# A causal convolution and a gated feed-forward block: the first convolution of blocks 4 and 5 moved from TensorE to ACT, DVE and POOL

## The chip, the cores and the metric

The kernel runs on one core of a Trainium2 chip. The metric is the device time of one execution in microseconds (us), median of several runs. The engines are called TensorE (PE in the profile, with its weight loads as PEld), VectorE (DVE), ScalarE (ACT), GpSimd (POOL) and SyncE (SP, which only issues DMAs here).

## What is computed

A softmax over 7 taps for each of 8 heads, a causal depthwise convolution of x (8 sequences of 4096 tokens, 192 channels, each head's taps on its 24 channels), and a gated feed-forward block with 1536 hidden units on the result.

```python
w = np.exp(weight - weight.max(-1, keepdims=True))
w = w / (w.sum(-1, keepdims=True) + 1e-09)                  # 8 heads x 7 taps
x_pad = np.concatenate([zeros(B, 6, D), x], axis=1)
out[b, s, h] = sum(w[h, k] * x_pad[b, s + k, h] for k in range(7))
g = out @ w_gate                                           # 192 -> 1536
val = out @ w_val
y = (g / (1 + np.exp(-g)) * val) @ w_out                   # 1536 -> 192, 32768 tokens
```

## The kernel before

**Blocks, steps and bursts.** The 32768 tokens are 64 blocks of 512; four blocks are a unit (16 units). A block takes 12 steps, one for each 128 hidden units, so there are 768 steps n, with block b = n // 12 and j = n % 12. `gate_val(n)` (L734) issues six matmuls (L743): gate in the upper 64 rows of the array and val in the lower 64, three pieces k = 0, 1, 2 of 64 channels each. They read the block's three input tiles `xc[b]` (channels by tokens, the two halves of each tile hold different channels, since gate and val walk the channels in different order). ACT makes `sig` = silu of gate (L752), and DVE multiplies it by val to `h` (L754). Gate and val have three PSUM buffers each (`ppool`, bufs=3).

The third product is made in bursts of 24 matmuls (`slot`, `down`, L769), four bursts k = 1 to 4 to a block, a burst after every third step. Each row half of the array adds into one of two PSUM banks; `swap` says which half takes which bank, and where the halves trade banks the burst waits for an earlier silu (`after`). Burst 4 is followed by the copies of both banks (ACT L820, DVE L821) and the store.

**Two ways to the convolution.** The first blocks are convolved on TensorE, since they are wanted at once: blocks 0 and 1 alone (`early`), blocks 2 and 3 as a pair (`early_pair(2)` at step 19) and blocks 4 and 5 as a pair (`early_pair(4)` at step 27): 64 small matmuls (L394) of windows of x (`xp`) with a band of taps, whose result is tokens by channels and is cast by ACT and DVE to `tme` (L411). It must then be turned to channels by tokens: blocks 0, 1 and 2 by TensorE (`eturn`, L457, copies at L470), blocks 3, 4 and 5 through DRAM (`eout` stores, L429; `efetch` reads with DMA transposes, L439).

All later blocks are convolved channel-major by ACT, DVE and POOL. `cast_x` (L542, a POOL DMA) writes a unit's x as fp16 to a DRAM scratch `xs`; `turn_x` (L560) reads it back with DMA transposes on SP, two a block: `x01` holds channels 0 to 127, `x12` channels 64 to 191. `join_x` (L569) puts the third 64 channels of two blocks into one tile. A pair of blocks makes three jobs (`conv_job`, L580): "block" i, "pair" (channels 128 to 191 of both) and "block" i + 1. In a job ACT makes tap 0 (`total`) and taps 3 and 4 (`part`, L643), DVE adds taps 1 and 2 to `total` (L618), and POOL, after DVE's last, adds the parts, makes taps 5 and 6 (`piece`, L608) and adds them (L593).

`pooled_work(n, j)` (L708) issues these after each step from two lists, `dve_steps` and `act_steps`: one DVE instruction and one or two ACT taps at j = 1, 7, 10, where ACT is at most three jobs ahead; one more ACT tap stands at j = 4 ahead of the burst. When all jobs of a block are done, `place` (L653) issues four SP DMAs that put the channels where gate and val want them (`pxc`), 14 steps after the jobs or 16 before the block, whichever is later.

**What sets the order.** `seq` keeps the instructions of each engine, and the DMAs of each issuing engine, in the order in which the program issues them; a DMA waits in its queue for its data, and what stands behind it waits too. The steps at which casts, transposes and jobs are issued are written out by hand in `planned(v)` (L678): `head` and `cast` for the DRAM scratch, `times` for the transposes and the join, `jobs` for the queueing of the jobs. In step n the order is `gate_val`, the burst, the early work, `pooled_work`, the planned work.

## Time and profile before

| what | us |
|---|---|
| three runs | 771.16, 771.73, 771.82 |
| median | 771.73 |
| the profiled execution | 771.32 |
| its span, first to last instruction | 769.5 |
| TensorE's granted clock over the span | 1.000 |

The page is read by engine: how long each was busy and in what share of the span. A line of a group gives line, engine, operation, tiles and shapes, count, busy time and mean length, and behind the bar the idle time of the engine before it and what ended that:

```
L754 DVE TENSOR_TENSOR h<-sig,val 128x512 f16<-128x512 f16 x768 | 497.1, 682 | 59.4 <-PE gate L743 54.3
L752 ACT ACTIVATE sig<-gate 128x512 f16<-128x512 f32 x768 | 457.5, 596 | 107.9 <-PE gate L743 78.3
L593 POOL TENSOR_TENSOR total<-total,part 128x512 f32<-128x512 f32 x174 | 221.8, 1275 | 73.8 <-DVE total L618 50.0
L618 DVE SCALAR_TENSOR_TENSOR total<-x,both_taps,total 128x512 f32<-128x512 f16 x174 | 186.2, 1070 | 0.0
L643 ACT ACTIVATE part<-x,both_taps 128x512 f32<-128x512 f16 x174 | 124.3, 714 | 0.0
L394 PE MATMUL cv<-xp,band 64*32 64x120 f16 x128 | 1.8, 216 | 0.4 <-DVE h L754 0.2 <-issue 0.2
```

In a line of a stretch of time stand its bounds, its length, then for PE, PEld, DVE, ACT and POOL the busy time with the number of instructions, the clock, the DMA engines' mean share and GB/s. In a timeline stand start, length, engine, line, operation, tiles, and in brackets the idle time before it and what ended it. In the table of DMA issues the last number is the median time from issue to landing.

### The profile page before, as it was taken

The numbers are of one execution on the slowest core, as the hardware profiler recorded it, in microseconds if no ns is written. First come the engines' busy times: TensorE is split into PE (matmuls) and PEld (weight loads), VectorE is DVE, ScalarE is ACT, GpSimd is POOL, SyncE is SP. The second block draws the span as 40 slices with busy tenths as digits, with TensorE's granted clock in tenths as the row PEclk, the third lists the DMA queues.
The fourth block names the chain that finished last, engine by engine and source line by source line (L and its number), as shares of the span: only waits on it lengthen the run. The fifth ranks groups of instructions, "written<-read, shape, count | busy, mean of one in ns | idle before, by whom it ended". The sixth has DMA issues, their size and how long they took to land.

```text
span 769.5 us, 27729 instructions
## 1 busy us (share of the span) xinstructions
PE 763.0 (99%) x11041; PEld 616.1 (80%) x11041; DVE 702.5 (91%) x1048; ACT 649.1 (84%) x1114; POOL 637.8 (83%) x570
## 2 busy tenths in 40 slices
PE   8999999999999999999999999999999999999997
PEld 5878888888888888888888888888888888888886
DVE  7789999999999999999999999999999999999875
ACT  6688888888888888888888888888888888888764
POOL 8039899999989898998989989999899998889700
PEclk9999999999999999999999999999999999999999
DMA  9966646653536444456443545447454453121211
GB/s 143 198 115 122 154 80 149 128 88 84 123 81 124 106 85 108 99 95 119 92 102 89 100 111 108 92 82 118 92 120 101 82 116 92 53 70 37 71 56 43
DMA packets 145762, 77.52 MB, mean 101 GB/s; under 512 B 79976, under 2 KB 145504, under 8 KB 145632
## 3 DMA queue, kind: packets, MB, share of 16 engines
q1 hardware_dynamic: 126720, 61.05, 34.3%
q0 software_dynamic: 18912, 14.70, 13.8%
q8 instruction: 86, 1.41, 0.8%
q14 instruction: 44, 0.36, 0.2%
HBM read 29.39 MB, written 37.46 MB: 87 GB/s over the span
## 4 chain that ended last, share of the span: by engine, by line
PE 99%; ACT 0%; DVE 0%; issue 0%
PE val L743 51%; PE acc L769 33%; PE gate L743 14%; PE warm L837 0%; PE turn L457 0%; PE acc L790 0%; PE cv L394 0%; PE cv L350 0%; ACT tme L368 0%; DVE h L754 0%; ACT wide L308 0%; ACT o_sb L899 0%; PE taps L295 0%; DVE spread L275 0%; PE ctap L513 0%
## 5 line engine op out<-in xcount | busy, mean ns | idle before, releaser
L754 DVE TENSOR_TENSOR h<-sig,val 128x512 f16<-128x512 f16 x768 | 497.1, 682 | 59.4 <-PE gate L743 54.3
L752 ACT ACTIVATE sig<-gate 128x512 f16<-128x512 f32 x768 | 457.5, 596 | 107.9 <-PE gate L743 78.3
L743 PE MATMUL gate<-pxc,w 64*128 64x512 f16 x2088 | 488.0, 376 | 0.0
L743 PE MATMUL val<-pxc,w 64*128 64x512 f16 x2088 | 488.0, 376 | 0.0
L743 PEld LDWEIGHTS <-w 64*128 64x128 f16 x4608 | 360.1, 110 | 119.7 <-issue 0.7
L769 PE MATMUL acc<-wo,h 64*128 64x192 f16 x6096 | 336.7, 243 | 0.0
L769 PEld LDWEIGHTS <-h 64*128 64x128 f16 x6096 | 311.6, 94 | 21.4 <-ACT sig L752 0.4
L593 POOL TENSOR_TENSOR total<-total,part 128x512 f32<-128x512 f32 x174 | 221.8, 1275 | 73.8 <-DVE total L618 50.0
L618 DVE SCALAR_TENSOR_TENSOR total<-x,both_taps,total 128x512 f32<-128x512 f16 x174 | 186.2, 1070 | 0.0
L608 POOL TENSOR_SCALAR piece<-x,both_taps 128x512 f32<-128x512 f16 x174 | 159.7, 918 | 0.0
L593 POOL TENSOR_TENSOR total<-total,piece 128x512 f32<-128x512 f32 x87 | 123.5, 1419 | 7.3
L643 ACT ACTIVATE part<-x,both_taps 128x512 f32<-128x512 f16 x174 | 124.3, 714 | 0.0
L593 POOL TENSOR_TENSOR pxc<-total,piece 128x512 f16<-128x512 f32 x58 | 74.2, 1279 | 4.8
L643 ACT ACTIVATE total<-x,both_taps 128x512 f32<-128x512 f16 x87 | 62.1, 714 | 0.0
L743 PE MATMUL gate<-xc,w 64*128 64x512 f16 x216 | 51.4, 377 | 0.0
L743 PE MATMUL val<-xc,w 64*128 64x512 f16 x216 | 51.3, 376 | 0.0
L593 POOL TENSOR_TENSOR y<-total,piece 128x512 f16<-128x512 f32 x29 | 36.8, 1271 | 2.4
L821 DVE COPY o_sb<-acc 128x384 f32<-128x384 f32 x63 | 34.5, 548 | 0.0
L820 ACT COPY o_sb<-acc 128x384 f32<-128x384 f32 x63 | 29.6, 471 | 2.6 <-PE acc L769 2.6
L549 POOL DMA_DIRECT2D xs<-in_x_dram x15 | 11.7, 778 | 0.0
L837 PE MATMUL warm<-fill 128*128 128x512 f16 (+1 forms) x12 | 4.1, 500 | 1.0 <-DVE fill L90 1.0
L470 ACT COPY xc<-turn 128x520 f16<-128x520 f16 (+1 forms) x5 | 2.9, 588 | 1.0 <-PE turn L457 0.9
(66 smaller groups left out, 55.8 us busy)
## 6 DMA issues: line engine op xcount, KB each, us to landing
out_dram<-o_sb SPq DMA_DIRECT2D x63, 384.0 KB
pxc<-pxc SPq DMA_DIRECT2D x116, 64.0 KB
pxc<-y SPq DMA_DIRECT2D x116, 64.0 KB
xs<-in_x_dram POOLq DMA_DIRECT2D x7, 774.0 KB, 8.6
xs<-in_x_dram POOLq DMA_DIRECT2D x7, 768.0 KB, 7.0
x<-x SPq DMA_DIRECT2D x29, 66.0 KB
x<-xs SPq DMA_TRANSPOSE x116
xp<-in_x_dram POOLq DMA_DIRECT2D x4, 240.0 KB, 7.5
```

Source lines behind the costliest of these rows:

```text
L549: nc.gpsimd.dma_start(out=flat[skip * D : rows * D].rearrange("(a n) -> a n", n=n), in_=bass.AP(tensor=x_flat.tensor, offset=(t0 - XP + sk ...
L593: nc.gpsimd.tensor_tensor(job["dst"] if k == K - 1 else total, total, part, op=ALU.add)
L608: nc.gpsimd.tensor_scalar(part, shifted(k), scalar1=job["tap"][:, k : k + 1], scalar2=1.0, op0=ALU.mult, op1=ALU.mult,)
L618: nc.vector.scalar_tensor_tensor(job["total"], shifted(k), job["tap"][:, k : k + 1], job["total"], op0=ALU.mult, op1=ALU.add,)
L643: nc.scalar.activation(part, shifted(k), AF.Copy, scale=job["tap"][:, k : k + 1])
L743: nc.tensor.matmul(o, w16[m][p0 : p0 + Q, k, e::E], xc[b][k][p0 : p0 + Q, 0:TB], start=(k == 0), stop=(k == SL - 1),)
L752: silu[n] = seq(nc.scalar.activation(sg, g, AF.Silu)).ins
L754: seq(nc.vector.tensor_tensor(hj, sg, v, op=ALU.mult))
L769: nc.tensor.matmul(acc[b][bank][:, s, :], hj[p0 : p0 + Q, ts(2 * bank + s, P)], wo16[p0 : p0 + Q, j, :], start=(not second and j == 0 and ...
L820: seq(nc.scalar.copy(o_sb[:, 0:2, :], acc[b][0]))
L821: seq(nc.vector.tensor_copy(o_sb[:, 2:4, :], acc[b][1]))
L837: nc.tensor.matmul(warm[:, 0:width], fill, fill.unsqueeze(1).to_broadcast([P, width // P, P]), start=True, stop=True, skip_group_check=True,)
```

## The change

Blocks 4 and 5 take the channel-major way. `early_pair(4)`, its `xp` tile with loads and copies, `eout(4)`, `eout(5)`, `efetch(4)` and `efetch(5)` are gone. Unit 1 is cast in two parts (`part_of`): blocks 4 and 5 with a cast at step 11, transposes at 16 to 19 and jobs queued at 18; blocks 6 and 7 with a cast at 23, transposes at 30 to 34 and jobs at 35. Units 2 and 3 move too (casts from 12 to 32 and from 56 to 62, jobs from 40 to 55 and from 56 to 82). The join stands ahead of the last transpose of a pair.

In a job POOL now makes tap 5 (`rest`) when ACT makes tap 0, adds ACT's parts to it as they come, adds tap 6 and at the end adds `total` and `rest`; its number of products and adds is the same. For the first two jobs (`soon`) ACT makes two taps at j = 7 and j = 10. The hand-over is issued in two parts, "block" and "pair", each 4 steps after its job. The bursts of block 0 stand at steps 9, 12, 14 and 17 instead of 9, 12, 15 and 17, with other bank halves in the last two and other waits.

```diff
@@ -182,11 +182,10 @@
     for m in range(3):
         load_wo(m)
     xp = {}
-    for e in (2, 4):
-        xp[e] = cpool.tile([P, 4 * EG, D], fp16, tag="xp", name="xp")
-        for r in range(2):
-            windows(xp[e], Q * r, (e + r) * TB, CO, 0, 4 * EG)
-        twice(xp[e])
+    xp[2] = cpool.tile([P, 4 * EG, D], fp16, tag="xp", name="xp", bufs=1)
+    for r in range(2):
+        windows(xp[2], Q * r, (2 + r) * TB, CO, 0, 4 * EG)
+    twice(xp[2])
 
     pq_i = small("pq_i", [P, 1], i32)
     seq(nc.vector.tensor_single_scalar(pq_i, pid, 15, op=ALU.bitwise_and))
@@ -434,7 +433,7 @@
     def efetch(b):
         xc[b] = []
         for k in range(SL):
-            t = cpool.tile([P, XW], fp16, tag=f"xc{k}", name=f"xc{k}", bufs=8)
+            t = cpool.tile([P, XW], fp16, tag=f"xc{k}", name=f"xc{k}", bufs=4)
             seq(
                 nc.sync.dma_start_transpose(
                     out=t[:, 0:TB], in_=scre[b][0:TB, Q * k : Q * k + P]
@@ -523,26 +522,27 @@
         for m, name in enumerate(pick):
             taps[name] = both_taps[:, m * K : m * K + K]
 
-    def first_of(u):
-        return HALF if u == 1 else 0
-
-    def head_x(u):
-        rows = XP + UT - first_of(u) * TB
-        xs[u] = dpool.tile([rows, D], fp16, tag="xs", name="xs")
+    def part_of(u, i):
+        return (u, i // HALF * HALF, HALF) if u == 1 else (u, 0, UB)
+
+    def head_x(part):
+        u, i0, n = part
+        xs[part] = dpool.tile([XP + n * TB, D], fp16, tag=f"xs{n}", name="xs")
...
-    def cast_x(u):
-        t0 = u * UT + first_of(u) * TB
-        rows = XP + u * UT + UT - t0
-        flat = xs[u].rearrange("t d -> (t d)")
+    def cast_x(part):
+        u, i0, n = part
+        t0 = u * UT + i0 * TB
+        rows = XP + n * TB
+        flat = xs[part].rearrange("t d -> (t d)")
...
@@ -580,38 +581,30 @@
     def conv_job(u, what, i):
         index = n_jobs[0]
         n_jobs[0] += 1
-        on_act, on_pool = SHARES[index % len(SHARES)]
-        job = {"dve": len(ON_DVE), "act": len(on_act), "parts": []}
+        job = {"dve": len(ON_DVE), "act": len(ON_ACT)}
         at = XP - pad
 
         def shifted(k):
             return job["src"][:, at + k : at + k + TB]
 
-        def add(part, k):
-            total = job["total"]
-            seq(
-                nc.gpsimd.tensor_tensor(
-                    job["dst"] if k == K - 1 else total, total, part, op=ALU.add
-                )
-            )
+        def add(to, one, two):
+            seq(nc.gpsimd.tensor_tensor(to, one, two, op=ALU.add))
+
+        def product(k):
+            tag = "rest" if k == ON_POOL[0] else "piece"
+            part = cpool.tile([P, TB], fp32, tag=tag, name=tag, bufs=2)
+            seq(
+                nc.gpsimd.tensor_scalar(
+                    part, shifted(k), scalar1=job["tap"][:, k : k + 1],
+                    scalar2=1.0, op0=ALU.mult, op1=ALU.mult,
+                )
+            )
+            return part
 
         def proceed():
-            if job["dve"]:
-                return
-            while job["parts"]:
-                add(*job["parts"].pop(0))
-            if job["act"]:
-                return
-            for k in on_pool:
-                part = cpool.tile([P, TB], fp32, tag="piece", name="piece", bufs=2)
-                seq(
-                    nc.gpsimd.tensor_scalar(
-                        part, shifted(k), scalar1=job["tap"][:, k : k + 1],
-                        scalar2=1.0, op0=ALU.mult, op1=ALU.mult,
-                    )
-                )
-                add(part, k)
-            finished[u, what, i] = step_now[0]
+            if job["dve"] == 0 and job["act"] == 0:
+                add(job["dst"], job["total"], job["rest"])
+                finished[u, what, i] = step_now[0]
 
         def dve_step(k):
             seq(
@@ -637,96 +630,115 @@
                 )
                 dve_steps.extend((index, lambda k=k: dve_step(k)) for k in ON_DVE)
             else:
-                part = cpool.tile([P, TB], fp32, tag="part", name="part", bufs=8)
-                job["parts"].append((part, k))
+                part = cpool.tile([P, TB], fp32, tag="part", name="part", bufs=4)
             seq(
                 nc.scalar.activation(
                     part, shifted(k), AF.Copy, scale=job["tap"][:, k : k + 1]
                 )
             )
-            if k != FIRST:
-                job["act"] -= 1
-                proceed()
-
-        act_steps.extend((index, lambda k=k: act_step(k)) for k in (FIRST, *on_act))
-
-    def place(u, i):
+            if k == FIRST:
+                job["rest"] = product(ON_POOL[0])
+                return
+            add(job["rest"], job["rest"], part)
+            job["act"] -= 1
+            if job["act"] == 0:
+                for k in ON_POOL[1:]:
+                    add(job["rest"], job["rest"], product(k))
+            proceed()
+
+        act_steps.extend((index, lambda k=k: act_step(k)) for k in (FIRST, *ON_ACT))
+
+    sides = {}
+
+    def place(u, i, what):
         b = UB * u + i
-        for k in (1, 2):
-            xc[b].append(
+        if b not in sides:
+            sides[b] = [
                 cpool.tile([P, XW], fp16, tag=f"pxc{k}", name=f"pxc{k}", bufs=4)
-            )
-        t0, t1, t2 = xc[b]
-        y = y2[u, i // 2][Q * (i % 2) : Q * (i % 2) + Q, :]
-        for dst, src in (
-            (t1[0:Q, 0:TB], t0[Q:P, 0:TB]),
-            (t1[Q:P, 0:TB], y),
-            (t2[0:Q, 0:TB], y),
-            (t2[Q:P, 0:TB], t0[0:Q, 0:TB]),
-        ):
-            seq(nc.sync.dma_start(out=dst, in_=src))
+                for k in (1, 2)
+            ]
+        t1, t2 = sides[b]
+        if what == "block":
+            t0 = xc[b][0]
+            xc[b] += sides[b]
+            moves = (t1[0:Q], t0[Q:P]), (t2[Q:P], t0[0:Q])
+        else:
+            y = y2[u, i // 2][Q * (i % 2) : Q * (i % 2) + Q, :]
+            moves = (t1[Q:P], y), (t2[0:Q], y)
+        for dst, src in moves:
+            seq(nc.sync.dma_start(out=dst[:, 0:TB], in_=src[:, 0:TB]))
 
     plan = {}
     placing = []
 
-    def queue_jobs(u):
-        for i in range(first_of(u), UB, 2):
+    def queue_jobs(part):
+        u, i0, n = part
+        for i in range(i0, i0 + n, 2):
             for job in (("block", i), ("pair", i // 2), ("block", i + 1)):
                 conv_job(u, *job)
-        placing.extend((u, i) for i in range(first_of(u), UB))
-
-    def planned(v):
+            placing.extend(
+                (u, m, what)
+                for m, what in (
+                    (i, "block"), (i, "pair"), (i + 1, "pair"), (i + 1, "block")
+                )
+            )
+
+    def planned(part):
+        v, i0, n = part
         s0 = ustep * v
         turns = [
             turn
-            for i in range(first_of(v), UB, 2)
-            for turn in ((i, 0), (i, Q), (i + 1, Q), (i + 1, 0), (i // 2, None))
+            for i in range(i0, i0 + n, 2)
+            for turn in ((i, 0), (i, Q), (i + 1, Q), (i // 2, None), (i + 1, 0))
         ]
-        if v == 1:
-            head, cast, jobs = 10, 11, 27
-            times = (20, 20, 20, 23, 23)
+        if v == 1 and i0 == 0:
+            head, cast, jobs = 10, 11, 18
+            times = (16, 16, 16, 18, 19)
+        elif v == 1:
+            head, cast, jobs = 10, 23, 35
+            times = (30, 30, 31, 33, 34)
         elif v == 2:
-            head, cast, jobs = 10, 12, 40
-            times = (32, 33, 34, 35, 37, 38, 39, 40, 41, 43)
+            head, cast, jobs = 10, 32, 55
+            times = range(47, 57)
         elif v == 3:
-            head, cast, jobs = 56, 56, 56
-            times = range(66, 86, 2)
+            head, cast, jobs = 62, 62, 82
+            times = range(74, 94, 2)
         else:
             head = cast = s0 - (115 if v > 4 else 100)
             jobs = s0 - 89
             first = s0 - (95 if v > 4 else 87)
             times = range(first, first + 20, 2)
-        plan.setdefault(head, []).append(lambda: head_x(v))
-        plan.setdefault(cast, []).append(lambda: cast_x(v))
+        plan.setdefault(head, []).append(lambda: head_x(part))
+        plan.setdefault(cast, []).append(lambda: cast_x(part))
         for m, turn in enumerate(turns):
             def todo(i=turn[0], at=turn[1]):
                 join_x(v, i) if at is None else turn_x(v, i, at)
 
             plan.setdefault(times[m], []).append(todo)
-        plan.setdefault(jobs, []).append(lambda: queue_jobs(v))
+        plan.setdefault(jobs, []).append(lambda: queue_jobs(part))
 
     def pooled_work(n, j):
         step_now[0] = n
+        ready = dve_steps[0][0] if dve_steps else None
+        if ready is not None and j in (1, 7, 10):
+            dve_steps.pop(0)[1]()
         if j != 4:
-            ready = dve_steps[0][0] if dve_steps else None
-            if j in (1, 7, 10) and ready is not None:
-                dve_steps.pop(0)[1]()
-            for _ in range(2 if j == 10 and n // NCH % 2 == 0 else 1):
+            many = (j == 10 and n // NCH % 2 == 0) or (
+                act_steps and act_steps[0][0] < soon and j != 1
+            )
+            for _ in range(2 if many else 1):
                 ahead = act_steps[0][0] if act_steps else n_jobs[0]
                 if j in (1, 7, 10) and act_steps and (
                     ready is None or ahead < ready + 3
                 ):
                     act_steps.pop(0)[1]()
         while placing:
-            u, i = placing[0]
-            need = (u, "block", i), (u, "pair", i // 2)
-            if not all(job in finished for job in need):
-                break
-            done = max(finished[job] for job in need)
-            if n < max(done + 14, ustep * u + NCH * i - 16):
+            u, i, what = placing[0]
+            done = finished.get((u, what, i if what == "block" else i // 2))
+            if done is None or n < done + 4:
                 break
             placing.pop(0)
-            place(u, i)
+            place(u, i, what)
 
     hbuf = {}
     silu = {}
@@ -812,10 +824,12 @@
             down(b, [(True, G[0])], 0, after)
             down(b, [(True, G[1])], 0, None)
         elif k == 3:
-            down(b, [(False, G[2])], 1, after)
-            down(b, [(False, G[3])], 1, None)
+            swap = 0 if b == 0 else 1
+            down(b, [(False, G[2])], swap, after)
+            down(b, [(False, G[3])], swap, None)
         else:
-            down(b, [(True, G[2]), (True, G[3])], 0, after)
+            swap = 1 if b == 0 else 0
+            down(b, [(True, G[2]), (True, G[3])], swap, after)
             o_sb = hpool.tile([P, SUBS, D], fp32, tag="o_sb", name="o_sb", bufs=3)
             seq(nc.scalar.copy(o_sb[:, 0:2, :], acc[b][0]))
             seq(nc.vector.tensor_copy(o_sb[:, 2:4, :], acc[b][1]))
@@ -851,8 +865,10 @@
     early(0, (gate_bank, gate_bank, val_bank))
     eturn(0, (*acc_banks, gate_bank), make_channel_taps)
     make_band()
-    for v in range(1, NU):
-        planned(v)
+    planned(part_of(1, 0))
+    planned(part_of(1, HALF))
+    for v in range(2, NU):
+        planned(part_of(v, 0))
 
     for n in range(n_steps):
         b, j = divmod(n, NCH)
@@ -861,9 +877,9 @@
             early(1, (*acc_banks, gate_bank))
         elif n == 8:
             eturn(1, (gate_bank, val_bank))
-        elif n in (9, 12, 15, 17):
-            k = {9: 1, 12: 2, 15: 3, 17: 4}[n]
-            slot(k, 0, silu[n - 1 if k == 4 else n - 2])
+        elif n in (9, 12, 14, 17):
+            k = {9: 1, 12: 2, 14: 3, 17: 4}[n]
+            slot(k, 0, None if k == 3 else silu[n - 2])
         elif j % 3 == 1 and n > 18:
             if j == 4 and act_steps and act_steps[0][0] < (
                 dve_steps[0][0] if dve_steps else n_jobs[0]
@@ -871,18 +887,14 @@
                 act_steps.pop(0)[1]()
             k = {1: 3, 4: 4, 7: 1, 10: 2}[j]
             slot(k, b - 1 if j < 7 else b, silu[n - 2])
-        if n in (19, 27):
-            early_pair(2 if n == 19 else 4)
+        if n == 19:
+            early_pair(2)
         elif n == 20:
             eout(3)
         elif n == 21:
             eturn(2, (gate_bank, val_bank))
         elif n == 22:
             efetch(3)
-        elif n in (28, 29):
-            eout(n - 24)
-        elif n in (30, 36):
-            efetch(4 if n == 30 else 5)
         pooled_work(n, j)
         for job in plan.pop(n, ()):
             job()
```

## The prediction, made before the change had run

> **What bounds the kernel now.** I read, in order: the page's busy times and chain of waits (which engine sets the end), the stretches of time (where that engine has gaps), then the timelines of TensorE, ScalarE and VectorE around the two steps at which the pairs of early blocks are made, the DMA queue of SyncE there, and the table of DMA issues (how long a cast takes to land).
>
> ```profile
> span 769.5 us, 27729 instructions
> PE 763.0 (99%) x11041; PEld 616.1 (80%) x11041; DVE 702.5 (91%) x1048; ACT 649.1 (84%) x1114; POOL 637.8 (83%) x570
> PE 99%; ACT 0%; DVE 0%; issue 0%
> 20.00:40.00 20.00, 19.56 (x382) 15.78 (x380) 14.93 (x26) 13.76 (x24) 0.00 (x0) 1.00 0.97 191
> 40.00:60.00 20.00, 20.00 (x294) 16.23 (x290) 17.97 (x30) 17.36 (x31) 9.70 (x9) 1.00 0.54 112
> xs<-in_x_dram POOLq DMA_DIRECT2D x7, 774.0 KB, 8.6
> xs<-in_x_dram POOLq DMA_DIRECT2D x7, 768.0 KB, 7.0
> xs<-in_x_dram POOLq DMA_DIRECT2D x1, 390.0 KB, 10.5
> ```
>
> The chain is 99% TensorE, and from 40 us to 740 us it has no gap (20.00 busy of 20.00). So the time changes by what is taken out of TensorE's stream or put into it as a stall, and by nothing else. In the timelines (start, length, engine, line), TensorE first:
>
> ```profile
> 25.65 1.16 PE L769 MATMUL acc<-wo,h 64*128 64x192 f16 x24
> 30.11 0.40 PE L743 MATMUL gate<-xc,w 64*128 64x512 f16 x1
> 32.19 0.41 PE L743 MATMUL gate<-xc,w 64*128 64x512 f16 x1
> 32.34 0.37 PE L743 MATMUL val<-xc,w 64*128 64x512 f16 x1
> 36.79 0.38 PE L743 MATMUL gate<-xc,w 64*128 64x512 f16 x1
> 38.30 0.46 PE L394 MATMUL cv<-xp,band 64*32 64x120 f16 x33
> 39.00 0.40 PE L394 MATMUL cv<-xp,band 64*32 64x120 f16 x31 [0.24 <-DVE h L754]
> 41.10 0.38 PE L743 MATMUL gate<-xc,w 64*128 64x512 f16 x1
> 44.04 0.38 PE L743 MATMUL gate<-xc,w 64*128 64x512 f16 x1
> ```
>
> ```profile
> 29.54 1.21 ACT L411 CAST tme<-cv 128x480 f16<-128x480 f32 x2 [0.80 <-PE cv L394]
> 30.98 1.24 ACT L752 ACTIVATE sig<-gate 128x512 f16<-128x512 f32 x2 [0.23 <-PE val L743]
> 32.29 1.19 ACT L470 COPY xc<-turn 128x520 f16<-128x520 f16 x2
> 31.61 1.34 DVE L754 TENSOR_TENSOR h<-sig,val 128x512 f16<-128x512 f16 x2 [0.49 <-PE val L743]
> 33.35 3.83 SPq L566 DMA_TRANSPOSE x<-xs  x3
> ```
>
> The first gate matmul after a burst comes every 2.93 us (41.10 to 44.04): three steps of 0.648 and a burst of 0.99. From 36.79 to 41.10 it is 4.31. And val of step 22 starts at 32.34, just as h of step 20 ends (31.61 + 0.69 = 32.30): three PSUM buffers, one taken by the turn of block 2, so step 22 waits for step 20.
>
> [...]
>
> **Removed: early_pair(4), eout(4), eout(5), efetch(4), efetch(5).** From TensorE: 4.31 - 2.93 = **1.38 us** (64 small matmuls with their waits). Its casts (ACT 2 x 0.56, DVE 2 x 0.65 and 2 copies of 0.25), 8 stores and 6 transposes on SP and 2 loads and 2 copies of xp[4] lay beside TensorE: nothing, except that casts of x can start earlier.
>
> **Bursts 9, 12, 14, 17.** Before, the burst at step 17 waited for the silu of step 16 (25.00 + 0.60 = 25.60; burst at 25.65). First gates of steps 16 and 18 are 24.16 and 26.65, 2.49 apart; two steps and a burst are 2.28. Now it waits for step 15's, and the burst at 14 for none (the h of step 11 is done at 21.1, the burst would start at 22.5). **-0.21 us**; bounds 0 and -0.21.
>
> **First taps at step 19.** This is the cost. The conditions in pooled_work give, for the first jobs: ACT taps 0 and 3 of job 0 at 19, tap 4 and job 1's tap 0 at 22, one tap at 25, 28 and 31; DVE at 22, 25, 31, 34. At 19 the two taps stand on ACT behind the two tme casts and ahead of the silu of step 20. The casts end at 30.75, now 30.54. A tap keeps ACT 0.63 (start to start, 47.42 to 48.05; 0.75 in the slowest pair). Casts run 0.60 apart, so taps start at 30.58 and 31.21 and silu 20 at 31.84, where without them it would be 30.98 - 0.21 = 30.77: late by 1.07. Queued behind it are silu 21, the two copies of block 2's turn and silu 22; h of step 20 follows, and val of step 22 waits for that h, with no slack (above). So TensorE stalls at step 22 by **+1.07 us**. Bounds: 0 (were the wait hidden) to 1.5 (2 x 0.75). What is late next: copies at 33.0 to 34.2, ready for block 2 at step 24 (35.35); silu 22 at 34.2, then two more taps to 35.4+0.6, silu 23 at 36.0 instead of a due 35.5. Step 26 needs it at 37.6: covered. ACT has caught up by step 28.
>
> **Data for those taps.** xs of blocks 4 and 5: POOL issues its cast after two xp loads and four band copies, at 17.73 - 1.35 = 16.4 (two loads of 0.68 are gone). Landing: the slowest row is 10.5, so 26.9 at the latest; a transpose lands 2.6 us after its issue (33.35 to 35.9); 29.5 is before 30.58. Hidden, with a margin of 1.1 at the worst. On SP these transposes now stand ahead of the stores and fetches of block 3: with the cast at 26.9, three transposes to 30.8, the join after the third's landing to 32.7, the last transpose to 34.0, four stores (2.1) to 36.1, fetches after their landing (2.2) from 38.3 to 42.3, where before they ended at 42.3 too; landed at 44.9, block 3's step 36 is at 47.1. Covered.
>
> **The second half's cast (blocks 6, 7).** It is planned at step 23, and on POOL it stands behind job 0's add of tap 4 (ACT done 35.4), product, add and job 1's product: 1.3 + 1.1 + 1.4 + 0.9 from 35.5, so issued at 40.2. The turns stand on SP's queue from step 30 on and wait for it; behind them are the join and the hand-over of y to block 4 (step 38). Landing: by bytes from 774 KB in 8.6, of which 1.5 passes before the first packet, half is 5.0: 45.2; by the slow row, taken while the queue was full, 10.5: 50.7. In 40 to 50 us the queues are light (0.54 busy), so I take 5.0. A rule of the skill (DMA: Bandwidth & Descriptors, Anatomy of one DMA) gives 2.0 us and bytes over 436 GB/s: an estimate of 2.9, a landing at 43.1 and only a wider margin; no row here is that quick. First tap of block 6 is at step 37: silu 37 ends at 49.2 (step 25 at 36.0, four bursts of 2.93, 0.85 and 0.60); the transpose is there at 47.9. Covered by 1.3; ACT's idle of 0.4 and 0.9 of PSUM slack come on top. So nothing up to a cast of 7.6 us. Unit 2's cast, moved from step 12 to 32, leaves POOL at about 48 and lands 7.0 to 8.6 later, before its first turn (step 47, 57.6).
>
> **Hand-over to block 4.** Transposes 45.3 to 49.2 (1.29 each), join after the third has landed (50.5), one transpose to 52.3, two copies to 53.5, landed 1.9 to 3.7 later (the join issued at 43.69: most parts 45.6, the last 47.4): 55.4 to 57.2. Step 48 reads it at 59.0. Covered by 1.8 or more. y itself is out of POOL at about 50.
>
> **The rest.** 3 jobs more: 6 DVE instructions of 0.74 to 1.13, 9 taps, POOL 3 x 7.1 (48.34 to 55.46). The rates stay 3 DVE and 4.5 ACT per block; POOL has 21.3 us of work in 23.5. Jobs run on to step 739 instead of 721, before block 63 (756). The shortest lead from a hand-over to its block falls from 15 steps to 10 (9.8 us): four copies of 0.6 and 3.7 make 6.1; covered.
>
> **Sum.** -1.38 - 0.21 + 1.07 = **-0.52 us** from the profiled execution (771.32, a span of 769.5 and 1.8 around it): 770.80. That one lies 0.41 under the median of 771.73, whose like is predicted: **771.2**.
>
> **Rivals.** A, the taps cost nothing: ACT would find idle time. For it: ACT is 69% busy from 20 to 40 us. Against: no slack at step 22. 771.73 - 1.59 = 770.1. B, slower: the second cast lands late, ACT stands at step 37 on block 6's first tap, silus and h queue behind it and TensorE runs dry. It decides from a cast of 7.6 us on and costs what is above that: at 10.5, 2.9 us, so 771.2 + 2.9 = 774.1, and the hand-over to block 4 comes up to 0.9 late on top. For it: that row, and a queue order with two waits on SP; against: quiet queues then. C, POOL falls behind with the shorter lead: a late y would stall each even block; by 21.3 of 23.5 I leave it almost nothing. It would give 772 to 775.
>
> **How the numbers follow.** A measurement of this kernel tells about 0.2% (1.5 us) from no change. Forecast 0.68, all within. A 0.12: its 770.1 lies just past the bound (770.2), so 0.09 of it faster and 0.03 within. B 0.18, of which 0.01 within, and C 0.02. Together faster 0.09, same 0.72, slower 0.19. The forecast's own range is 770.1 to 771.8; with B's smaller half, 770.0 to 773.2.
>
> **What would show it.** Right: no cv matmuls after 31 us, first gates 2.93 apart from step 25 on; val of step 22 near 33.2 with silu 20 near 31.8; the burst of step 17 at about 25.45. Wrong: a first tap on ACT long after 30.6 (cast one late); a gap in TensorE near 50 us with ACT at L643 waiting for a DMA (B), or at 59 us with xc or pxc (hand-over); repeated gaps every 24 steps (C); no gap at step 22 (A).

## The result, and the profile after

| | us |
|---|---|
| before, median of 13 runs | 771.5 (771.11 to 771.82) |
| after, median of 13 runs | 773.8 (772.34 to 784.94) |
| ratio, with its 95% interval | 1.0033 (1.0024 to 1.0042) |
| predicted | 771.2 (770.0 to 773.2) |
| profiled execution of after; its span | 773.51; 771.7 |

The change makes the kernel slower by a third of a per cent. The 784.94 is one slow execution, which the ratio leaves out; the other twelve end at 775.79. The page of after:

```profile
span 771.7 us, 27633 instructions
PE 763.8 (99%) x10977; PEld 533.9 (69%) x10977; DVE 712.6 (92%) x1050; ACT 652.7 (85%) x1121; POOL 643.4 (83%) x587
PE 95%; POOL 2%; DMA 1%; ACT 0%; issue 0%; DVE 0%; SPq 0%; POOLq 0%; DVEq 0%
```

and its stretches of time (TensorE's busy time is the first number after the length, then PEld, DVE, ACT, POOL):

```profile
20.00:40.00 20.00, 19.21 (x328) 13.87 (x326) 15.42 (x26) 15.69 (x28) 6.23 (x6) 1.00 0.65 124
40.00:60.00 20.00, 19.83 (x288) 15.98 (x285) 19.83 (x28) 17.24 (x30) 18.92 (x18) 1.00 0.79 138
80.00:100.00 20.00, 19.05 (x268) 14.43 (x266) 18.97 (x26) 16.08 (x29) 16.30 (x15) 1.00 0.67 131
400.00:420.00 20.00, 20.00 (x294) 13.68 (x290) 18.19 (x29) 17.51 (x31) 17.80 (x17) 1.00 0.42 82
```

TensorE is still 95% of the chain (99% before), but it now has holes behind 40 us, where it had none. From 40 to 60 us VectorE is busy 19.83 of 20 (17.97 before) and GpSimd 18.92 (9.70 before).

Since the rhythm of TensorE is fixed where nothing waits, the difference can be put down step by step: for each of the 768 steps, the start of its first gate matmul after, less the same before. Where that difference changes, something happened. In us:

| step | change | what |
|---|---|---|
| 0 to 20 | +0.27 | first loads, and the pair at step 19 (-0.3 to +0.9 in the experiments, from run to run) |
| 18 | -0.21 | burst of step 17 earlier |
| 22, 23 | +1.02 | taps ahead of silu 20 |
| 28, 29 | -1.38 | the pair of blocks 4 and 5 is gone |
| 42, 50 | +0.36, +0.43 | h late on VectorE |
| 73 | +1.11 | y of block 6 late by DMA |
| 194, 242, ... 722 | +0.92 | 0.07 to 0.09 in every 48 steps, 12 times |
| end | -0.32 | |

The sum is 2.2, which is the difference of the spans. Four views show the rows that matter. Steps 22 and 23, TensorE with ScalarE and VectorE, in the timelines:

```profile
30.88 0.73 ACT L635 ACTIVATE total<-x,both_taps 128x512 f32<-128x512 f16 x1
31.50 0.72 ACT L635 ACTIVATE part<-x,both_taps 128x512 f32<-128x512 f16 x1
32.11 1.08 ACT L764 ACTIVATE sig<-gate 128x512 f16<-128x512 f32 x2
32.74 1.28 DVE L766 TENSOR_TENSOR h<-sig,val 128x512 f16<-128x512 f16 x2 [1.19 <-ACT sig L764]
33.48 0.37 PE L755 MATMUL val<-xc,w 64*128 64x512 f16 x1 [0.35 <-DVE h L766]
```

Two taps, silu of step 20 behind them, h behind that, and val of step 22 waiting for the h: as forecast.

Step 73, SyncE's queue and the stalled matmul:

```profile
72.63 2.57 SPq L567 DMA_TRANSPOSE x<-xs  x2
76.69 0.46 SPq L571 DMA_DIRECT2D x<-x  x1
77.20 1.64 SPq L567 DMA_TRANSPOSE x<-xs  x1
78.94 2.45 SPq L669 DMA_DIRECT2D pxc<-y  x4
84.84 0.37 PE L755 MATMUL gate<-pxc,w 64*128 64x512 f16 x1 [0.95 <-DMA pxc<-y]
```

The copies of y for block 6 stand behind unit 2's ten DMAs (one in each step from 47 to 56), whose second join (the x<-x line) waits for its transposes. Planned at step 62 (73.85 us), they go out at 78.94, and the matmul waits for them. The late issue is half of it. The second copy, issued at 79.52, lands at 84.80, after 5.28, and unit 3's cast runs beside it:

```profile
79.07 0.82 POOL L549 DMA_DIRECT2D xs<-in_x_dram  x1
```

The median of such copies is 2.6 (the DMA table), with which it would have landed at 82.1, ahead of step 72 (83.29).

Steps 42 and 50, GpSimd above, VectorE below:

```profile
48.57 0.76 POOL L549 DMA_DIRECT2D xs<-in_x_dram  x1
49.35 1.28 POOL L591 TENSOR_TENSOR y<-total,rest 128x512 f16<-128x512 f32 x1
50.60 2.95 POOL L591 TENSOR_TENSOR rest<-rest,part 128x512 f32<-128x512 f32 x2
```

```profile
50.03 2.38 DVE L611 SCALAR_TENSOR_TENSOR total<-x,both_taps,total 128x512 f32<-128x512 f16 x1
52.34 1.87 DVE L766 TENSOR_TENSOR h<-sig,val 128x512 f16<-128x512 f16 x3
53.07 0.37 PE L755 MATMUL val<-xc,w 64*128 64x512 f16 x1 [0.17 <-DVE h L766]
```

A tap of VectorE that lasts 0.74 alone lasts 2.38: it meets two adds of GpSimd, the second from 50.60 to 51.87, and ends 0.55 behind that one. The h behind it is late, and val of step 42 waits. Taps of 1.76 at 56.39 and 1.42 at 59.87, each held by one add, do the same to step 50.

The drift, at step 194 (VectorE, then GpSimd):

```profile
198.56 1.47 DVE L611 SCALAR_TENSOR_TENSOR total<-x,both_taps,total 128x512 f32<-128x512 f16 x1
199.96 1.87 DVE L766 TENSOR_TENSOR h<-sig,val 128x512 f16<-128x512 f16 x3
201.75 1.47 DVE L611 SCALAR_TENSOR_TENSOR total<-x,both_taps,total 128x512 f32<-128x512 f16 x1
203.14 1.87 DVE L766 TENSOR_TENSOR h<-sig,val 128x512 f16<-128x512 f16 x3
```

```profile
198.22 1.27 POOL L591 TENSOR_TENSOR rest<-rest,part 128x512 f32<-128x512 f32 x1
201.40 1.27 POOL L591 TENSOR_TENSOR rest<-rest,part 128x512 f32<-128x512 f32 x1
```

The second tap stands just ahead of h of step 191, which the burst at step 193 needs. It starts 0.35 into an add, ends 0.55 after it (203.22 and 202.67), and that h is late. In before the two taps at this place are shorter, and the h isn't late:

```profile
197.00 0.74 DVE L618 SCALAR_TENSOR_TENSOR total<-x,both_taps,total 128x512 f32<-128x512 f16 x1
199.90 1.15 DVE L618 SCALAR_TENSOR_TENSOR total<-x,both_taps,total 128x512 f32<-128x512 f16 x1
```

### The profile page after: what moved, and what is told of

Same layout as the page of the kernel before. It is cut to its first block, busy times and chain, and to the rows that moved or that the text cites. A ratio compares the mean times of both kernels' runs of the same rounds, so it can differ in the third digit from the quotient of the medians.

```text
span 771.7 us, 27633 instructions
## 1 busy us (share of the span) xinstructions
PE 763.8 (99%) x10977; PEld 533.9 (69%) x10977; DVE 712.6 (92%) x1050; ACT 652.7 (85%) x1121; POOL 643.4 (83%) x587
## 4 chain that ended last, share of the span: by engine, by line
PE 95%; POOL 2%; DMA 1%; ACT 0%; issue 0%; DVE 0%; SPq 0%; POOLq 0%; DVEq 0%
PE gate L755 58%; PE acc L781 32%; PE val L755 5%; DMA xe<-in_x_dram 1%; DMA pxc<-y 1%; POOL w L141 0%; POOL rest L591 0%; POOL xe L96 0%; DVE h L766 0%; PE acc L802 0%; ACT sig L764 0%; ACT tme L410 0%; ACT part L635 0%; PE cv L349 0%; POOL rest L597 0%
## 5 line engine op out<-in xcount | busy, mean ns | idle before, releaser
L755 PE MATMUL gate<-pxc,w 64*128 64x512 f16 x2160 | 505.0, 376 | 0.9 <-DMA pxc<-y 0.9
L755 PEld LDWEIGHTS <-w 64*128 64x128 f16 x4608 | 270.0, 110 | 172.9 <-issue 3.1
L781 PEld LDWEIGHTS <-h 64*128 64x128 f16 x6096 | 263.5, 94 | 53.5 <-DVE h L766 0.3
L781 PE MATMUL acc<-wo,h 64*128 64x192 f16 x6096 | 297.3, 243 | 0.1
L591 POOL TENSOR_TENSOR rest<-rest,part 128x512 f32<-128x512 f32 x180 | 239.1, 1328 | 13.5 <-ACT part L635 6.5
L591 POOL TENSOR_TENSOR rest<-rest,piece 128x512 f32<-128x512 f32 x90 | 119.2, 1324 | 7.5
L591 POOL TENSOR_TENSOR pxc<-total,rest 128x512 f16<-128x512 f32 x60 | 76.2, 1270 | 22.8 <-DVE total L611 10.9
L597 POOL TENSOR_SCALAR rest<-x,both_taps 128x512 f32<-128x512 f16 x90 | 77.7, 863 | 9.8 <-DMA x<-xs 9.3
L597 POOL TENSOR_SCALAR piece<-x,both_taps 128x512 f32<-128x512 f16 x90 | 75.4, 838 | 0.0
L591 POOL TENSOR_TENSOR y<-total,rest 128x512 f16<-128x512 f32 x30 | 38.1, 1269 | 41.3 <-ACT sig L764 22.2
```

The lines of the kernel that those rows point to most:

```text
L591: seq(nc.gpsimd.tensor_tensor(to, one, two, op=ALU.add))
L597: nc.gpsimd.tensor_scalar(part, shifted(k), scalar1=job["tap"][:, k : k + 1], scalar2=1.0, op0=ALU.mult, op1=ALU.mult,)
L755: nc.tensor.matmul(o, w16[m][p0 : p0 + Q, k, e::E], xc[b][k][p0 : p0 + Q, 0:TB], start=(k == 0), stop=(k == SL - 1),)
L781: nc.tensor.matmul(acc[b][bank][:, s, :], hj[p0 : p0 + Q, ts(2 * bank + s, P)], wo16[p0 : p0 + Q, j, :], start=(not second and j == 0 and ...
```

## The experiments

**First four: what each part costs.** The theories were late copies on SyncE and casts of x beside other DMAs against taps that are drawn out on VectorE. Each kernel is after (or before) with one edit.

e1, unit 2's DMAs every second step:

```diff
-            times = range(47, 57)
+            times = range(47, 67, 2)
```

> The changed kernel, with unit 2's eight transposes and two joins issued every second step (47, 49, ... 65) instead of every step (47 to 56). Late hand-over (H): in the changed kernel these ten DMAs keep SyncE busy from 61.3 to 78.8 us, so that y's copies for block 6, planned at step 62 (73.9 us), are issued at 78.9 and read at 83.5, where TensorE loses 1.11 us; spread out, the copies stand ahead of the second join and its last transposes, the loss at step 72 goes, and the median falls by about 1.1, with less scatter from run to run (772.3 to 775.8 before). Squeezed VectorE (V): the loss lies in VectorE's taps being drawn out by POOL's adds (2.38 us at 50.0, 1.83 once a unit): no change beyond 0.3.

Measured: 772.96, ratio 1.0019 (1.0010 to 1.0027). The copies for block 6 go out at 74.41 in place of 78.94, and 0.14 are lost at step 74 in place of 1.11 at step 73. Steps 42 (0.38), 50 (0.43) and the drift (1.12) stay. So without the ten DMAs in ten steps the stall at step 73 goes, and the other losses have another cause. But e1 changes two things for these copies: issued from 74.41 on, they have also landed (the second at 76.99) before unit 3's cast goes out at 79.25. e5 parts the two.

e2, the first taps one step later and one at a time (none at step 19, one at 20, two at 22, two at 31):

```diff
+        count = 0 if j not in (1, 7, 10) else 2 if j == 10 and n // NCH % 2 == 0 else 1
+        for _ in range({19: 0, 20: 1, 22: 2, 31: 2}.get(n, count)):
```

> The changed kernel, with no tap at step 19, one at 20 (behind silu 20 instead of ahead of it), two at 22 and two at 31, so that VectorE's taps and all jobs end where they did. Stall at step 22 (S): the two taps ahead of silu 20 cost TensorE 1.02 us at steps 21 to 23; without them at most 0.3 is left, and the median falls by 0.7 to 1.0. If the stall is made up for later by waits of the same size (at steps 42, 50 or 72), the median moves by less than 0.4.

Measured: 777.37, ratio 1.0082 (1.0061 to 1.0103). The 1.02 at steps 22 and 23 is gone (0.35 at step 26 is left), and 3.14 come at step 49 and some 6 at steps 73 to 76. The 3.14 and the 3.76 at step 73 are waits for the copies of y. The other 2.42, at steps 74 to 76, are no wait: behind the gap of 2.92 TensorE's granted clock was 0.50 from 88 to 94 us, and a matmul took 0.63 and not 0.38:

```profile
88.14 0.58 PE L749 MATMUL val<-pxc,w 64*128 64x512 f16 x1 [2.92 <-DMA pxc<-y]
92.24 0.63 PE L749 MATMUL gate<-pxc,w 64*128 64x512 f16 x1
```

After the gap of 2.35 at step 49 the clock stayed at 1.00. (This profiled execution took 780.74, 3.4 more than the median.) The join for blocks 6 and 7 went out at 56.87, behind a transpose issued at 48.50, which had the cast of unit 2 (49.14) beside it; in after such a transpose took 6.1, with no cast near it 2.8.

e3, before with the new bursts of block 0 alone:

> The kernel before, with only the bursts of block 0 at 9, 12, 14 and 17 and their bank halves as in the changed kernel. By the prediction's own term: 0.21 us faster than before, the first gate of step 18 2.28 after that of step 16 instead of 2.49. The rival is that the gain at step 18 is made up for at step 20, where the pair of blocks 2 and 3 is convolved: no change.

Measured: 771.44, ratio 0.9997 (0.9989 to 1.0006); step 18 shows -0.21, as in after. The time itself can't tell 0.21 from nothing.

e4, after with unit 3's cast at step 56 in place of 62:

> The changed kernel, with unit 3's cast back at step 56 instead of 62, so that its 774 KB are not moved while y's copies for block 6 are. The copies' landing is slow for the cast (C): the second copy, issued at 79.5, landed at 84.8, 5.3 us later where the median is 2.6; without the cast beside it it lands at about 82, before it is read at 83.5, and the loss of 1.11 at step 72 goes: about 1.1 faster. The late issue on SyncE alone decides (H): the copies still come late by 0.5 or more, or vary from run to run.

Measured: 774.27, ratio 1.0035 (1.0022 to 1.0048). The cast no longer ran beside the copies of y, but beside the transposes of unit 2's second join, which went out at 80.87 in place of 76.69; step 73 lost 1.34. With no cast beside them the copies themselves landed in 2.0 to 2.1, but they went out at 82.74. Moved by itself, the cast only changes what it disturbs.

**Second four: apart from each other.** e5 is e1 with unit 2's cast at step 36 and unit 3's at 68, so that no cast goes out while the DMAs of a hand-over are on their way:

```diff
-            head, cast, jobs = 10, 32, 55
+            head, cast, jobs = 10, 36, 55
-            head, cast, jobs = 62, 62, 82
-            times = range(74, 94, 2)
+            head, cast, jobs = 68, 68, 82
+            times = range(80, 100, 2)
```

> The kernel after with its casts of x kept out of the stretches in which the transposes before a join and the copies of y are in flight: unit 2's turns every second step from 47 (as in e1), its cast at step 36, unit 3's cast at step 68 with turns from 80. Collision theory (a transpose or copy that runs beside a cast of x lands in 6 to 8 us in place of 2.6): the step-73 stall, 1.11 in the kernel after and 0.14 in e1, is 0.05 or less, the last transpose of block 6 before its join lands in under 4 us, and the time is about 772.8. Rival (a crowded queue alone made the stall at 73, the casts are harmless): the join still waits 4 us or more, and the time is e1's 773.0. Both leave the steps 42 and 50 and the drift of 0.09 in 48 steps as they are.

Measured: 771.86, ratio 1.0005 (0.9996 to 1.0014). The stall at step 73 is gone, and not because the copies of y are early. They go out nearly as late as in after, and unit 3's cast only behind them:

```profile
78.38 2.46 SPq L669 DMA_DIRECT2D pxc<-y  x4
86.12 0.83 POOL L549 DMA_DIRECT2D xs<-in_x_dram  x1
```

The second, issued at 78.96, lands at 80.97, after 2.01 in place of 5.28, and nothing waits. So the stall was a late issue and a cast beside the copies, together. Those at 42 and 50 are gone as well, which I had not expected. The timelines of e5 show why for step 42:

```profile
49.30 1.27 POOL L591 TENSOR_TENSOR y<-total,rest 128x512 f16<-128x512 f32 x1
50.52 2.94 POOL L591 TENSOR_TENSOR rest<-rest,part 128x512 f32<-128x512 f32 x2
```

```profile
50.72 1.62 DVE L611 SCALAR_TENSOR_TENSOR total<-x,both_taps,total 128x512 f32<-128x512 f16 x1
```

Without the cast's 0.76 in GpSimd's queue the add of y is through before the tap starts, which then meets one add and not two. It is the alignment that counts and not the cast as such: in e2, with unit 2's cast at step 32 as in after and taps one step later, neither step loses. In part the expectation failed: the join for blocks 6 and 7 still waited 4.2 after the last transpose's issue, with no cast near it (3.5 in e6, 2.8 in e13; with one 5.0 in e1, 6.1 in after, 8.4 in e2). A cast makes transposes slower, but it isn't all that does; what else does stays open.

e6 is e5 with e2's taps:

> e5 with the first taps as in e2 (none at step 19, one at 20, two at 22 and at 31). e2 lost 3.1 us at step 49 and some 6 at steps 73 to 76, and gained about 1 us at step 22. Collision theory: those losses came from the casts of x beside the transposes and copies, so here both are under 0.3, the stall at step 22 stays away, and the sum is -1.38 - 0.21 + 0.35 + 0.3 + 12 x 0.09 = 0.1: about 771.7, level with before. Rival (taps that start later leave the blocks' conv late by themselves): a stall of 2 us or more stays near step 49 and again near 73, and the time is 774 to 777.

Measured: 771.69, ratio 1.0003 (0.9994 to 1.0012). Step 49 is clean, and of the 6 us near step 73 0.24 (step 66) and 0.43 (step 74) are left. So e2's losses were not the later taps' by themselves but came from the casts and the crowded queue, which e6 changes together. This kernel is 1.48 ahead of before at step 60; with those two steps and the drift (1.17), 0.36 behind at the end.

e7 is e1 with an add of GpSimd left out in each job:

```diff
-            add(job["rest"], job["rest"], part)
+            if k != 4:
+                add(job["rest"], job["rest"], part)
```

> e1 with one of GpSimd's adds left out in every job: the part of tap 4 is computed by ScalarE but not added, so the output lacks that tap in the blocks from 4 on. Theory of the drawn-out VectorE (its taps last 1.8 to 2.4 us where they run beside GpSimd's adds of two tensors, and h comes late): the stalls at step 42 (0.38) and step 50 (0.50) and the 0.09 in every 48 steps shrink to under half, the longest tap of VectorE falls below 2.0 us, and the time is 770.9 to 771.7. Rival (the stalls come from the number and order of instructions on VectorE and ScalarE, and the adds beside them do nothing): the same stalls as in e1 and 773.0.

Measured: 775.19, ratio 1.0043 (1.0029 to 1.0056): a miss. With one of GpSimd's six operations a job gone, VectorE's taps are shorter in the mean (0.96 against e1's 1.10), the longest is 1.81, and steps 42 and 50 lose nothing, as expected. But 0.09 to 0.15 are lost in every 24 steps from step 122 on, 3.52 in all against e1's 1.12, and 1.22 at step 49, a wait for y: the transposes beside unit 2's cast, which goes out at 44.10 here, took up to 8.4. Timeline of VectorE in e7 before step 194:

```profile
198.03 0.74 DVE L611 SCALAR_TENSOR_TENSOR total<-x,both_taps,total 128x512 f32<-128x512 f16 x1
200.97 1.79 DVE L611 SCALAR_TENSOR_TENSOR total<-x,both_taps,total 128x512 f32<-128x512 f16 x1
```

The missing add let the next one (200.94 to 202.21) fall squarely on the tap ahead of h of step 191. It isn't how much GpSimd does, but where its adds stand.

e8 is before without the pair of blocks 4 and 5, which read the tiles of blocks 2 and 3:

```diff
-        if n in (19, 27):
-            early_pair(2 if n == 19 else 4)
+        if n == 19:
+            early_pair(2)
-        elif n in (28, 29):
-            eout(n - 24)
-        elif n in (30, 36):
-            efetch(4 if n == 30 else 5)
+        elif n == 36:
+            xc[4], xc[5] = xc[2], xc[3]
```

> The kernel before without the convolution of blocks 4 and 5 on TensorE, its stores, and its transposes: blocks 4 and 5 read the tiles of blocks 2 and 3, so two blocks of the output are another's. Theory: the part removed was worth the 1.38 us that TensorE's stream lost at step 28, and all of it reaches the end: 771.6 - 1.4 = 770.2. Rival (a wait that the removal uncovers, or DMA traffic, takes a part back): 771 or more, with a new gap of TensorE behind step 29.

Measured: 770.45, ratio 0.9984 (0.9975 to 0.9992), -1.38 at steps 28 and 29 and no new wait. The medians are 1.32 apart: within the interval, the removed part reaches the end in full.

**Third four: the drift.** e9 is e6, e10 is after, each with VectorE's tap of step 10 of a block moved to step 11, so that it stands behind h of step 11; e11 is e9 with the second tap of step 22 at 24:

```diff
-        if ready is not None and j in (1, 7, 10):
+        if ready is not None and j in (1, 7, 11):
```

> e6 with VectorE's taps at every block's steps 1, 7 and 11 in place of 1, 7 and 10: the tap of step 10 stood in VectorE's order just ahead of h of step 11, which the burst at the next block's step 1 needs at once; now it stands behind it. Theory of the held tap (in the traces a tap that starts while a GpSimd operation runs ends 0.55 us after that operation, up to 1.8 long, and drags the h behind it): taps go on being held, up to 1.8 us, but the 0.09 in every 48 steps goes (under 0.03 each) and with it the 0.43 at step 74, so the time is 771.7 - 1.1 - 0.4 = 770.2. Rival (the drift comes from elsewhere, as GpSimd's total work or the DMA traffic of each unit): 0.09 stays in each 48 steps and the time is 771.7.

> The kernel after with nothing but VectorE's taps at steps 1, 7 and 11 of each block. Theory of the held tap: of after's 2.19 us the 0.92 of drift goes; the 1.02 at steps 22 and 23 and the 1.11 at step 73 (casts beside the copies of y) stay, the stalls at steps 42 and 50 change in size: about 772.6. Rival (the drift is not the tap's place): 773.5 to 773.8.

> e9 with the second tap of step 22 moved to step 24, so that no step of the start has two taps on ScalarE ahead of a silu. Theory (two taps at one step make one silu late by about one tap, 0.6 us, less what slack there is): the 0.35 at step 26 goes, and the time is e9's less 0.35, some 769.9, faster than before by 0.2 to 0.25%. Rival (the 0.35 is the wait of the eighth block's turn or of block 3's tiles): it stays, and the time is e9's.

Measured: 795.65 (1.0313, 1.0299 to 1.0327), 794.34 (1.0296, 1.0282 to 1.0310) and 797.34 (1.0332, 1.0318 to 1.0347). The remedy was wrong by far: 0.80 and 0.47 are lost in every 48 steps. (e11 loses another 5.7 at steps 49 to 52: a gap of 3.69 for y, and behind it a granted clock down to 0.50, as in e2.) In e9 a tap of 1.50 now delays the h of the block's first step, and val two steps on waits for its PSUM buffer:

```profile
185.26 1.50 DVE L610 SCALAR_TENSOR_TENSOR total<-x,both_taps,total 128x512 f32<-128x512 f16 x1
186.69 1.27 DVE L760 TENSOR_TENSOR h<-sig,val 128x512 f16<-128x512 f16 x2
187.41 0.37 PE L749 MATMUL val<-pxc,w 64*128 64x512 f16 x1 [0.28 <-DVE h L760]
```

Steps 1, 4, 7 and 10 are the last of three ahead of a burst, and the burst gives VectorE a gap of 0.99 for the tap. Step 11 is the first of three, with no gap behind it. e9 and e10 don't decide between the theories; they show the same hold at a worse place.

e12 is e6 with the casts of units 4 and later eight steps later:

```diff
-            head = cast = s0 - (115 if v > 4 else 100)
+            head = cast = s0 - (107 if v > 4 else 100)
```

> e6 with the casts of x of units 4 and later issued eight steps later (107 steps ahead of their unit in place of 115); VectorE's taps stay at steps 1, 7 and 10. The cast's issue holds GpSimd for 0.76 us once in 48 steps, and GpSimd's later adds move by 0.6. If that shift is what brings an add onto the tap ahead of h of step 11, the drift of 0.09 in 48 steps moves or changes (0 to 0.2) and the time is 770.6 to 773; if the drift has nothing to do with the cast's place, it stays 0.08 to 0.10 at the same steps (194, 242, ...) and the time is e6's 771.7.

Measured: 779.1, ratio 1.0096 (1.0083 to 1.0110), 0.73 to 0.81 at the same steps (146, 194, 242, ... 626) in place of 0.09. One number, the step of a DMA issue on GpSimd, changes the drift by a factor of seven (8.61 against 1.17).

**Last six: the cast's place.** e13, e14 and e15 are e6 with 119, 123 and 127 in that line; e16 is e6 with the second tap of step 22 at step 24; e17 is e16 with 119; e18 is e17 with unit 3's cast at step 70 and its DMAs from 82.

> e6 with the casts of x of units 4 and later 119 steps ahead of their unit (115 in e6, 107 in e12). Theory: the drift is set by where GpSimd's adds stand against the one tap of VectorE ahead of h of step 11, and the cast's place shifts them; so the drift in 48 steps is again another number than 0.09 (0 to 0.3), and each 0.05 of it is 0.6 us of time: 770.6 at none, 771.7 at 0.09, 774.2 at 0.3. Where a step 194, 242, ... is held, the tap some 2 us earlier is longer than 1.1 us; where none is held, it is not. Rival: the drift stands at 0.09 again and the tap's length has nothing to do with it.

> As e13 with 123 steps. The cast is then issued eight steps further from the tap that was held in e6, and GpSimd has more time to catch up: by the theory the drift is smaller than e6's (0 to 0.09) and the time 770.6 to 771.7. Rival (any place gives some hold, as GpSimd is 19 of 20 us busy): 771.7 or more.

> As e13 with 127 steps: the drift 0 to 0.09 and 770.6 to 771.7 by the theory; 771.7 or more by the rival of e14.

> e6 with the second tap of step 22 moved to step 24. In e11, where VectorE's taps had been moved as well, the 0.35 at step 26 was gone, but 4 us were lost at step 49. Theory (the 4 us came from VectorE's taps between the h of one triple of steps): here the 0.35 goes too, step 49 stays clean, and the time is e6's 771.7 less 0.35: 771.35. Rival (a tap two steps later makes y of block 4 late by itself): 2 us or more at step 49 and 774 or more.

> e16 (casts of units 2 and 3 apart from the transposes and copies, first taps one at a time at steps 20, 22 and 24) with the casts of units 4 and later 119 steps ahead, as in e13. Theory: the terms add: e16's 771.16 less its drift of about 1.0, with e16's second cast issued 3.7 us earlier than in e13 so that no tap waits for it at step 41 (1.53 in e13's profiled run): 770.2, ratio about 0.998 to before. Rival (the drift and e16's start depend on each other, as a step later or earlier brings other adds onto the tap): 771 or more, with the drift back or a stall of over 1 us before step 100.

> e17 with unit 3's cast at step 70 and its turns from 82 on (68 and 80). What is left in e16 is 0.14 at step 90 and 0.44 at step 98, after taps of 1.5 to 1.9 us. If unit 3's cast shifts the adds that hold them, both change, to 0 or to another size up to 0.8, and the time is 769.7 to 770.6; if they come from the order of the jobs alone, both stay and the time is e17's.

| kernel | us, median | ratio (95%) | drift from step 110 on |
|---|---|---|---|
| e13, casts at 119 | 771.2 | 0.9993 (0.9984 to 1.0002) | 0.42 |
| e14, at 123 | 771.3 | 0.9999 (0.9990 to 1.0008) | 0.53 |
| e15, at 127 | 772.73 | 1.0017 (1.0008 to 1.0026) | 1.89 |
| e16, tap at 24 | 771.16 | 0.9993 (0.9984 to 1.0002) | 0.98 |
| e17, both | 770.66 | 0.9990 (0.9981 to 0.9999) | 0.50 |
| e18 | 772.84 | 1.0010 (1.0001 to 1.0018) | 0.52 |

(The drift of after is 0.92, of e6 1.17, of e12 8.61: each the difference to before at step 767 less that at step 110.) At 119 and 123 the drift is under half of e6's, at 127 over half as much again: the place sets it, but none of these took all of it. In e13's profiled execution step 41 lost 1.53 besides, by something close to what the forecast had as a rival: x late for the first tap of block 6. ScalarE there:

```profile
46.34 1.81 ACT L758 ACTIVATE sig<-gate 128x512 f16<-128x512 f32 x3
50.54 0.72 ACT L634 ACTIVATE total<-x,both_taps 128x512 f32<-128x512 f16 x1 [2.40 <-DMA x<-xs]
```

Its cast went out at 40.1 us on GpSimd. That alone doesn't make it late: e6, e12, e14 and e15, the same program up to step 113, send it at 40.2 to 40.9, and step 41 loses nothing. In e13 the cast landed after 6.22 (5.3 to 5.7 there), and the first transpose behind it after 4.15 (2.54 in e6); what held the transpose isn't shown. In e16 and e17, with one tap less at step 22, the cast goes out at 36.4 and 36.3. In e16 the 0.35 at step 26 is gone, as expected, but 0.19 came at step 30. e17 is the one version with the whole output that is faster than before by more than its interval, by 0.1%. It was expected at 770.2; half of the drift stayed, and 0.16, 0.29 and 0.42 at steps 62, 66 and 74.

Which steps lose this, the runs don't decide. e17 loses at 66 and 74, e16 and e18 at 90 and 98 (0.14 and 0.43 to 0.44). e6, e12, e14 and e15 lose 0.21 to 0.24 at 66 and 0.42 to 0.43 at 74, and e13 nothing; but e6 and e13, and e16 and e17, are the same program up to step 121, so their traces differ there by chance and not by an edit, and a profile is one execution. Why e18's median lies 2.2 above e17's isn't seen in its profiled execution either (a span of 769.6, near its fastest run). Both stay open.

What settles the drift is a comparison of five traces at the same place, the tap behind step 190. The tap's end is counted from the first gate of step 193:

| kernel | the two taps last | end of the second | step 194 comes later by |
|---|---|---|---|
| before | 0.74, 1.15 | 0.30 | 0 |
| e13 | 1.23, 1.47 | 0.63 | 0 |
| after | 1.47, 1.47 | 0.87 | 0.07 |
| e7 | 0.74, 1.79 | 0.94 | 0.13 |
| e12 | 2.13, 1.48 | 1.43 | 0.62 |

Up to some 0.81 there is no loss; above it each 0.1 us of a late tap is 0.1 us of the kernel. I had expected no long tap where there is no loss; e13 shows 1.47 without one. What counts is the end, to which both taps add: the second starts 0.85 ahead of that gate behind a first of up to 1.23, 0.60 ahead behind one of 1.47, 0.05 ahead behind 2.13. The rule isn't fitted to five places only. In fourteen traces (before, after, e1, e4 to e7 and e12 to e18), at the first burst of each of blocks 10 to 60, 714 places with a tap, the next step is late by the tap's end less 0.81, or not at all where it ends sooner, each time to within 0.03. It gives step 50 of after too (1.24, 0.43 lost), and steps 74 and 98 above (1.23 to 1.24, 0.42 to 0.44 lost).

## Why the prediction was wrong

**Right to a hundredth of a us:** the pair removed (-1.38 by the step table, -1.38 again in e8 alone) and the bursts (-0.21 at step 18, again in e3, where the time is too coarse to confirm it). **Right in mechanism, nearly in size:** the taps at step 19, 1.07 forecast, 1.02 measured, by the very chain of waits that it named. The data for those taps was hidden, as forecast. Those three make -0.57; the forecast's own sum was -0.52. What failed is what it had costed at nothing, or hadn't looked at.

**"Unit 2's cast, moved from step 12 to 32 ... lands 7.0 to 8.6 later, before its first turn."** True and beside the point. That step asked whether the cast is in time for its own reader, not what it and its ten DMAs do to others. They stand ahead of the copies of y for block 6 on SyncE, with a join that waits in the midst, and so the copies go out beside unit 3's cast, whose move from step 56 to 62 the forecast doesn't mention: 1.11 at step 73, 0.14 when the DMAs are spread (e1), none when the cast is elsewhere too and the copies go out late all the same (e5). And the cast's 0.76 on GpSimd pushed an add onto a tap of VectorE: 0.36 at step 42, and 0.43 at step 50, both gone in e5 (for step 50 the chain from the cast isn't followed up). Sum of this step: 1.90 where the forecast had 0. **"Covered by 1.8 or more"** for the hand-over to block 4 held, but barely: the join was taken at 50.5 and came at 54.15, since the transpose before it needed 6.1 and not 2.6; the copies landed at 58.7 and 58.9 and were read from 59.4 on. In e2 that cover was gone, and 3.1 us with it. So the 2.6 for a transpose, read at one place, was too small a term as well; 0.5 of the cover was left.

**"6 DVE instructions of 0.74 to 1.13 ... the rates stay"** took the length of a tap as given. It is in fact decided by what GpSimd does at that moment, and the bounds were too narrow: 0.74 to 2.38. The price is the drift of 0.92, and the trace of before would have shown the rule: its 29 taps that met one add and nothing else but a DMA's issue last 0.78 to 1.53 and all end 0.55 to 0.56 after it. That GpSimd's new order of adds (the parts as they come) set them anew against the taps is likely but not shown: before casts units 4 and later at the same steps and has no drift, and no run parts the new order from the three jobs more, which move all later jobs. The view by groups hides this, the two engines' timelines side by side show it.

**The rivals.** A (taps free) fell. B (the second half's cast late) didn't happen in after; in e13 x was late for that tap and cost 1.53, but of the 2.0 by which the tap came later than in e6 the cast has 0.4 and the transpose behind it 1.6. C (GpSimd behind, late y in even blocks) had the right engine and the wrong mechanism, and 0.02 of the chance: GpSimd wasn't behind, it was in the way. Late y came by SyncE and by the cast beside it. That B's 774.1 and C's 772 to 775 lie near the measured 773.8 is luck. The prediction's claim that a cast of 390 KB takes 5.0 by bytes was near: 5.02 for that cast, 6.28 for the other. The Trainium skill (DMA: Bandwidth & Descriptors, Anatomy of one DMA) would give an estimate of 2.9 there, which no row supports.

## What to carry to other kernels

When a transfer is moved, ask of every queue that it passes who stands behind it, and not only whether it is in time itself; a wait inside a row of ten DMAs holds all that come after, and what comes late may then meet another transfer (here 5.28 us for a copy that lands in 2.0 without the cast). Where VectorE and GpSimd work on SBUF together, read their two timelines side by side: a mean length is no price for an instruction whose length the other engine sets, and less work on GpSimd can cost time if its adds then fall at a worse moment. In a pipeline with no slack, a slip of 0.08 us at one place that returns with every unit is worth nearly as much (0.92 here) as one stall of a whole us.

## What the hardware showed that I had not expected

**A tap that meets a GpSimd operation waits for its end, to the hundredth.** In after 41 taps (two inputs in SBUF) met one add that was running, or began within 0.02, when they started, and of GpSimd nothing else but the issue of a DMA: they end 0.54 to 0.56 after it, however long that is; 30 that met nothing last 0.74 to 0.75. All 174 taps of before and 179 of the 180 of after end, to within 0.03, at the later of two times: 0.74 after their start, or 0.55 after the end of the add or product that was running then. The one left is the tap of step 42, which two adds held. It works the other way round as well: an add that began 0.12 after a tap lasted 1.76 in place of 1.27, and GpSimd's product, 0.69 alone, lasts 1.13 to 1.24 when it starts during a tap. The h product of VectorE, whose val lies in PSUM, lasts 0.67 to 0.69 in all 768 cases, 464 of which started during an add. The Trainium skill (SBUF — State Buffer, SBUF: two separate sides) states that the two engines share a pair of ports as an exclusive lock, held for a whole instruction by whichever starts first, where the VectorE instruction has two SBUF inputs and the GpSimd instruction reads SBUF; the traces agree, and give the price, up to 1.1 us for one add and 1.6 for two.

**A wait can cost more than itself.** With the gaps of 2.92 (e2) and 3.69 (e11) TensorE's granted clock fell to 0.50, for some 6 and 4 us, which cost another 2.4 and 1.7; with those of 2.35 (e2) and 0.95 (after) it stayed at 1.00.

**The share of weight loads doesn't follow the time here.** PEld fell from 80% to 69% of the span, with as many loads of the same mean length (4608 of 110 ns and 6096 of 94 in both pages), while the kernel became slower and TensorE stayed gapless from 400 to 420 us (20.00 of 20.00 in both).
